# A distance table made on VectorE instead of by GpSimd's iota, constant warm-up operands, diagonals shared with ScalarE, and a new order

## The chip, the cores and the metric

The kernel runs on one core of one Trainium2 chip. The time is the device time of one launch in microseconds (us), given as the median of the runs. Engines are named as in the profile: PE (TensorE matmul), PEld (its weight load), DVE (VectorE), ACT (ScalarE), POOL (GpSimd), SP (SyncE).

## The reference

Local attention with a few global keys and a distance bias, over q, k, v of shape (4, 8, 768, 64), and then a token-mixing layer over its output, of shape (4, 768, 512):

```python
scores = scale * np.matmul(q, k.transpose(0, 1, 3, 2))
rel = pos[:, None] - pos[None, :]
is_global = pos[None, :] < 8
is_local = (rel >= 0) & (rel < 96)
keep = is_global | is_local
dist = np.where(is_global & ~is_local, 96.0, np.abs(rel))
slopes = 2.0 ** (-8.0 * (np.arange(H) + 1) / H)
scores = np.where(keep, scores - slopes * dist, -1e9)
x = softmax(scores) @ v                      # heads side by side: (4, 768, 512)

theta = x @ w_theta
y = w_tok_r @ (x * cos(theta)) + w_tok_i @ (x * sin(theta))    # over tokens
u = x + y
out = u + np.maximum(u @ w_ch, 0)
```

## The kernel before

Tokens are cut into six tiles of 128, heads into four pairs. A query tile meets only its own key tile and the one before, in which the eight global keys replace the first eight columns (`kG` for K, `vG` for V). For each batch and pair the steps are: `q`/`qq` transposes of Q and K on PE and `qe` copies out of PSUM (on ACT or DVE, as the order says), `kg` (L360, L361), `s` scores on PE (L409), `e` the exponential on ACT (L421), `v` the product with V on PE (L468), whose 65th column is a column of ones and so gives the row sum, and `n`, reciprocal and multiplication on DVE (L479, L481). `xt` or a DMA transposes the result. The second half follows per batch: `th` (theta, L534), `sn` (cosine and sine on ACT, L544 and L546), `z` (products on DVE, L555), `m` (token mixing on PE, L568), `u`, its transpose, `c` (L617), `r` (L627) and the stores.

The bias enters in two ways. In batch 0 it is added by PE before the scores: `sb` (L382, L389) multiplies `diag`, the identity times a head's slope (L148), by `dist`, a table of 128 by 6 by 128 distances. In the later batches the exponential is multiplied on DVE by `etab`, a table of exp(-slope * distance) that ACT makes per head (`bt`, L153); so all eight tables are needed only from batch 1 on.

`dist` and `ident` come from `near`, whose element (p, j) is j - p. In the kernel before, GpSimd writes `near` with an iota (L106). VectorE makes `ident` (L120) and, in `distances` (L127 to L135), `far`, then `near` with the masked places put far away, their maximum as `dist`, two copies of it and the places of the global keys. `swap` (L141, L142) makes `distS`, `dist` with its halves swapped.

Batch 0 is loaded at the start. The first pair of heads comes in f32 over SP's and ACT's queues (L103, into `qk32`) and is cast by ACT and DVE (`cast`, L288). The rest comes over GpSimd's queue, which casts on the way: q and k of heads 2 and 3, then of 4 and 5, then V of heads 0 to 3 (`vn`, L92), q and k of 6 and 7, then V of heads 4 to 7. `vn` has 65 columns per head and tile: the loads write 64, and a memset on DVE writes the column of ones (L112). Before the loads of later batches the same memset stands as `mv` (L212).

PE also runs warm-ups (`warm`, L237): matmuls of a tile of zeros, written by DVE (L109), whose results nothing reads.

Nothing is scheduled by a program when the kernel is built. A text, `order`, names every step after the start in one sequence (L641 to L706), and each engine runs its own steps in that sequence; `banks` gives the PSUM bank of each. The start of the kernel (L101 to L157) stands in the order of the source. A build then adds the waits that the reads and writes of each tile ask for. An engine's instructions start in their order, so one that waits holds all behind it on its engine.

Of the kernel before, what the change touches and what calls it, by code (L numbers as in the profile page):

```python
# [16 lines left out]
def kernel(  # L17
# [47 lines left out]
    loads = {}  # L65
# [40 lines left out]
    nc.gpsimd.iota(near, pattern=[[1, 2 * T]], base=0, channel_multiplier=-1,  # L106
                   allow_small_or_imprecise_dtypes=True)
    zero = const.tile([T, 512], BF)
    nc.vector.memset(zero, 0.0)  # L109
    alloc_qk(0)  # L110
    alloc_v(0)
    nc.vector.memset(loads[0][1][:, :, :, D:D + 1], 1.0)  # L112
# [11 lines left out]
    far = const.tile([T, 2 * T], FP)  # L124
# [122 lines left out]
    @op  # L247
    def diag_(p):
        diagonals(p)
# [386 lines left out]
    def do(op, *a):  # L636
# [10 lines left out]
        s.0.1.2 sb.1.1 e.0.1.0 kg.0.2.0.4.v s.0.1.1 lw.2 vg.0.0.4 sb.2.0 e.0.1.2 sb.2.1 s.0.2.1
        e.0.1.1 v.0.0.0.0.6 s.0.2.0 n.0.0.0.0.6 lq.1.0.8 q.0.3.1 e.0.2.0 q.0.3.0 qe.0.3.1.v.2
        v.0.0.1.0.6 qe.0.3.0.a.2 sb.2.2 n.0.0.1.0.6 sb.3.0 e.0.2.1 v.0.1.0.0.6 kg.0.3.0.4.v
        v.0.1.1.0.6 n.0.1.0.0.6 s.0.2.2 sb.3.1 e.0.2.2 vg.0.4.4 s.0.3.0 s.0.3.1 e.0.3.0 n.0.1.1.0.6  # L650
        v.0.2.1.0.6 v.0.2.0.0.6 e.0.3.1 lw.4 n.0.2.1.0.6 v.0.3.2.0.2 xt.0.1.0.6 xt.0.0.0.6
        n.0.3.2.0.2 v.0.3.2.2.4 xe.0.0.0.6.a n.0.2.0.0.6 sb.3.2 s.0.3.2 xe.0.1.0.6.v e.0.3.2
        xt.0.2.0.6 xt.0.3.0.2 th.0.0.4 xe.0.2.0.6.v xe.0.3.0.2.a n.0.3.2.2.4 lc th.0.0.5 mv.1
        xt.0.3.2.4 v.0.3.2.4.6 xe.0.3.2.4.v th.0.0.3 n.0.3.2.4.6 th.0.1.2 sn.0.0.0 lv.1.4.4 sn.0.0.1
        xt.0.3.4.6 th.0.1.3 xe.0.3.4.6.v ww.0 sn.0.1.0 lv.1.0.4 ww.1 we.0.0.v th.0.2.2 we.1.0.v
        sn.0.1.1 z.0.0.1 lq.2.0.8 we.1.1.a th.0.2.3 z.0.0.0 ww.2 we.0.1.v ww.3 we.2.0.a z.0.1.1
        m.0.1.0 we.2.1.a z.0.1.0 m.0.0.0 sn.0.2.0 we.3.1.v m.0.2.0 sn.0.2.1 z.0.2.0 m.0.0.1 sin.0
        z.0.2.1 m.0.1.1 pc.1.0.0 m.0.0.2 pc.1.1.0 we.3.0.v bt.7 m.0.1.2 bt.2 pc.1.0.1 pc.1.1.1
        qq.1.0 u.0.0 qq.1.1 qe.1.0.1.a.2 u.0.1 m.0.3.0 qe.1.1.1.a.2 kg.1.0.0.4.v ud.0.1 ut.0.0
        qe.1.0.0.v.2 m.0.3.1 qe.1.1.0.a.2 ue.0.0.a kg.1.1.0.4.v s.1.0.0 pc.1.2.0 s.1.0.1 e.1.0.0  # L660
        pc.1.2.1 ww.4 pc.1.3.0 m.0.2.2 we.4.0.v e.1.0.1 we.4.1.v s.1.1.0 x.1.0.0 qq.1.2 e.1.1.0
        s.1.0.2 x.1.0.1 m.0.3.2 e.1.0.2 x.1.1.0 m.0.2.1 qe.1.2.1.a.2 u.0.3 s.1.1.1 mv.2 qe.1.2.0.a.2
        s.1.1.2 pc.1.3.1 m.0.4.0 kg.1.2.0.4.v lv.2.0.8 e.1.1.2 x.1.0.2 u.0.2 e.1.1.1 s.1.2.0 s.1.2.2
        m.0.4.2 x.1.1.2 e.1.2.0 x.1.1.1 lq.3.0.4 m.0.4.1 e.1.2.2 x.1.2.0 ut.0.2 ww.5 u.0.4 ue.0.2.a
        qq.1.3 we.5.1.a x.1.2.2 s.1.2.1 c.0.2.2 vg.1.0.8 we.5.0.a c.0.1.2 e.1.2.1 r.0.2.2
        v.1.0.2.0.6 qe.1.3.0.a.2 x.1.2.1 ut.0.3 qe.1.3.1.a.2 n.1.0.2.0.6 m.0.5.0 kg.1.3.0.4.a ut.0.4
        v.1.2.2.0.6 r.0.1.2 xd.1.0 ue.0.3.a v.1.1.2.0.6 n.1.2.2.0.6 ue.0.4.a s.1.3.0 c.0.3.2 e.1.3.0
        pc.2.1.0 pc.2.0.0 n.1.1.2.0.6 m.0.5.2 bt.6 s.1.3.1 r.0.3.2 s.1.3.2 e.1.3.1 xt.1.2.0.6
        x.1.3.0 xt.1.1.0.6 m.0.5.1 e.1.3.2 x.1.3.1 c.0.0.2 xe.1.2.0.6.a x.1.3.2 pc.2.1.1
        xe.1.1.0.6.a v.1.3.2.0.6 pc.2.0.1 u.0.5 qq.2.0 n.1.3.2.0.6 qq.2.1 qe.2.0.0.a.2 c.0.4.2  # L670
# [6 lines left out]
        ud.1.1 qe.2.2.0.a.2 u.1.0 s.2.1.1 vg.2.0.8 s.2.0.1 s.2.0.2 m.1.2.2 e.2.0.2 kg.2.2.0.4.v
        e.2.1.1 m.1.2.1 x.2.1.0 e.2.0.1 s.2.2.0 u.1.2 s.2.1.2 c.0.5.2 x.2.0.2 e.2.1.2 ud.1.2 x.2.1.1
        m.1.3.0 e.2.2.0 r.0.5.2 pd.3.2.1 s.2.2.2 x.2.0.1 qq.2.3 e.2.2.2 s.2.2.1 x.2.1.2 m.1.3.2
        e.2.2.1 st.0.2.2 x.2.2.2 pd.3.1.0 v.2.1.2.0.6 qe.2.3.0.a.2 m.1.5.0 n.2.1.2.0.6 qe.2.3.1.a.2  # L680
        v.2.0.2.0.6 kg.2.3.0.4.a x.2.2.0 xd.2.1 m.1.5.1 n.2.0.2.0.6 s.2.3.1 s.2.3.0 m.1.5.2 x.2.2.1
        e.2.3.0 xd.2.0 m.1.3.1 e.2.3.1 u.1.5 v.2.2.2.0.6 u.1.3 c.1.1.2 kg.3.0.0.4.v n.2.2.2.0.6
        m.1.4.0 x.2.3.0 s.3.0.0 s.2.3.2 ud.1.3 r.1.1.2 m.1.4.2 e.2.3.2 x.2.3.1 e.3.0.0 c.1.2.2
        xd.2.2 x.2.3.2 kg.3.1.0.4.a v.2.3.2.0.6 m.1.4.1 pd.3.2.0 n.2.3.2.0.6 c.1.3.2 u.1.4 xd.2.3
        th.2.0.0 vg.3.0.4 th.2.1.0 r.1.3.2 st.0.3.2 th.2.0.6 ud.1.0 th.2.2.0 th.2.0.3 st.1.3.2
        th.2.1.6 sn.2.0.0 pd.3.3.1 th.2.2.6 sn.2.0.1 th.2.1.3 z.2.0.0 c.1.0.2 st.0.1.2 sn.2.1.0
        z.2.0.1 pd.3.3.0 th.2.2.3 m.2.1.0 sin.3 sn.2.1.1 z.2.1.0 ud.1.4 m.2.0.0 sn.2.2.0 z.2.1.1
        m.2.2.0 r.1.2.2 st.1.1.2 sn.2.2.1 z.2.2.0 m.2.1.1 st.0.4.2 r.1.0.2 m.2.2.1 z.2.2.1
# [61 lines left out]
```

## Time and profile before

| what | value |
|---|---|
| median of 3 runs | 162.62 us (161.27 to 163.02) |
| the profiled execution: its time | 162.9 us |
| its span, first to last instruction | 160.7 us |
| mean granted TensorE clock | 0.999 |
| bytes moved by DMA | 25.49 MB, mean 159 GB/s |

Busy time by stage, in us of the engine's own time:

| stage (us) | PE | DVE | ACT | POOL |
|---|---|---|---|---|
| 0 to 10 | 7.82 | 6.30 | 6.25 | 9.19 |
| 10 to 20 | 9.37 | 8.78 | 8.90 | 5.38 |
| 20 to 30 | 9.38 | 7.51 | 9.22 | 5.20 |
| 30 to 40 | 9.79 | 8.79 | 9.11 | 0.88 |
| 60 to 70 | 9.95 | 9.67 | 9.04 | 5.90 |
| 70 to 80 | 8.92 | 9.90 | 8.06 | 3.68 |
| 140 to 150 | 9.95 | 4.04 | 0.00 | 0.00 |
| 150 to 161 | 7.30 | 5.69 | 0.59 | 0.00 |

A row of the timeline gives the start and the length in us, the engine, the line of the kernel, the operation with the tile that it writes and the tiles that it reads, their shape, and how many instructions are merged in it. Brackets give the idle time of the engine before it and what ended that time. In the list of waits a row names who waited for whom: us in total, times, and the longest. [...]

### The profile page before, as it was taken

What the parts mean: (1) busy time and instruction counts of PE and PEld (TensorE: products, weight loads), DVE (VectorE), ACT (ScalarE), POOL (GpSimd) and SP (SyncE); (2) the same over time, 40 slices, a digit from 0 to 9 for tenths busy, and PEclk for the clock granted to TensorE, in tenths of its full rate; (3) what the DMA queues carried; (4) which work ended last, traced back from release to release, by engine and by line L of the source; (5) the groups of instructions that cost most, each with busy time, mean ns of one, the idle gap of its engine ahead of it and who ended that gap; (6) DMA issues with size and microseconds to landing.
All of it is one profiled execution on the core that took longest, in us unless ns stands there. A gap on an engine that the chain in (4) does not pass through costs nothing.

```text
span 160.7 us, 4144 instructions
## 1 busy us (share of the span) xinstructions
PE 151.4 (94%) x1717; PEld 82.5 (51%) x1741; DVE 124.8 (78%) x263; ACT 107.4 (67%) x141; POOL 38.4 (24%) x46
## 2 busy tenths in 40 slices
PE   5989989999999999997999999999999999999991
PEld 1355774645546757444456554445465544444470
DVE  7578895897999999999998874697799715733492
ACT  3879898998999887998697391988963057200010
POOL 7985435400049320993000000000000000000000
PEclk9999999999999999999999999999999999999999
DMA  4999999999999999999998456953263470098376
GB/s 140 208 171 176 206 209 205 204 208 205 156 165 203 184 143 147 134 129 154 157 128 206 93 98 147 229 167 63 57 191 64 85 197 4 0 364 193 65 263 227
DMA packets 73553, 25.49 MB, mean 159 GB/s; under 512 B 61376, under 2 KB 70848, under 8 KB 73536
## 3 DMA queue, kind: packets, MB, share of 16 engines
q0 software_dynamic: 45712, 12.45, 84.5%
q1 hardware_dynamic: 27120, 12.00, 33.5%
q10 hardware_dynamic: 704, 0.79, 1.4%
q8 instruction: 13, 0.21, 0.5%
q14 instruction: 4, 0.03, 0.1%
HBM read 25.69 MB, written 6.29 MB: 199 GB/s over the span
## 4 chain that ended last, share of the span: by engine, by line
PE 80%; DVE 13%; issue 2%; ACT 2%; POOL 0%; DVEq 0%; POOLq 0%
PE bank L568 37%; PE bank L617 12%; PE bank L534 10%; PE bank L468 6%; PE bank L409 6%; PE bank L312 3%; PE bank L382 2%; DVE kT L337 2%; DVE x_sb L481 2%; DVE zri L555 2%; DVE qkn L344 1%; PE bank L498 1%; DVE o L627 1%; PE bank L237 1%; PE bank L303 1%
## 5 line engine op out<-in xcount | busy, mean ns | idle before, releaser
L568 PE MATMUL bank<-zri,w_tokT 128*128 128x512 bf16 x273 | 66.6, 379 | 2.1 <-DVE zri L555 1.0
L421 ACT ACTIVATE e<-bank 128x1024 bf16<-128x1024 f32 (+1 forms) x48 | 42.9, 959 | 8.9 <-PE bank L409 7.6
L568 PEld LDWEIGHTS <-w_tokT 128*128 128x128 bf16 x288 | 26.5, 98 | 30.9 <-issue 1.4
L555 DVE TENSOR_TENSOR zri<-x_sb,cs 128x1024 bf16<-128x1024 bf16 (+1 forms) x30 | 16.5, 579 | 9.6 <-ACT cs L546 7.2
L617 PE MATMUL bank<-w_ch_bf,uT 128*128 128x512 bf16 (+1 forms) x103 | 23.6, 355 | 0.3
L534 PE MATMUL bank<-w_theta_bf,xT 128*128 128x512 bf16 x93 | 22.5, 379 | 0.2
L627 DVE SCALAR_TENSOR_TENSOR o<-bank,u 128x512 f32<-128x512 f32 (+1 forms) x27 | 16.7, 625 | 6.0 <-PE bank L617 5.8
L576 DVE TENSOR_TENSOR u<-x_sb,bank 128x512 bf16<-128x512 bf16 x24 | 16.4, 682 | 4.1 <-PE bank L568 4.1
L546 ACT ACTIVATE cs<-bank,halfpi 128x1024 bf16<-128x1024 f32 x8 | 8.9, 1112 | 12.3 <-PE bank L534 12.1
L481 DVE TENSOR_TENSOR x_sb<-bank,rec 128x768 bf16<-128x768 f32 (+2 forms) x21 | 16.1, 767 | 0.7
L430 DVE TENSOR_TENSOR e<-e,etab 128x1024 bf16<-128x1024 bf16 (+1 forms) x24 | 14.6, 619 | 1.5 <-ACT e L421 1.2
L617 PEld LDWEIGHTS <-uT 128*128 128x128 bf16 x108 | 10.1, 98 | 9.3
L409 PE MATMUL bank<-qT,kT 64*128 64x128 bf16 x224 | 14.0, 218 | 0.5 <-DVE kT L337 0.3
L534 PEld LDWEIGHTS <-xT 128*128 128x128 bf16 x96 | 9.1, 98 | 10.2 <-DMA xT<-x_sb 0.3
L92 POOL DMA_DIRECT2D vn<-in_v_dram x6 | 10.2, 1708 | 16.9 <-DVE kG L361 13.7
L468 PEld LDWEIGHTS <-e 128*128 128x128 bf16 x352 | 12.6, 97 | 3.3 <-issue 0.8
L606 ACT COPY uT<-bank 128x512 bf16<-128x512 bf16 x5 | 2.9, 592 | 17.1 <-PE bank L592 17.0
L468 PE MATMUL bank<-vn,e 128*128 128x65 bf16 x224 | 13.3, 193 | 0.0
L409 PEld LDWEIGHTS <-kT 64*128 64x128 bf16 x224 | 8.8, 94 | 8.5 <-issue 6.9
L409 PE MATMUL bank<-qT,kG 64*128 64x128 bf16 x128 | 10.8, 216 | 0.4 <-DVE kG L361 0.4
L468 PE MATMUL bank<-vG,e 128*128 128x65 bf16 x128 | 10.3, 193 | 0.4 <-DVE vG L445 0.4
L433 DVE TENSOR_TENSOR e<-e,etab 128x1024 bf16<-128x1024 bf16 x12 | 8.2, 684 | 0.5 <-ACT e L421 0.3
(79 smaller groups left out, 185.2 us busy)
## 6 DMA issues: line engine op xcount, KB each, us to landing
out_dram<-o SPq DMA_DIRECT2D x21, 256.0 KB, 2.4
vn<-in_v_dram POOLq DMA_DIRECT2D x4, 384.0 KB, 16.0
qk<-in_q_dram POOLq DMA_DIRECT2D x2, 768.0 KB, 20.4
qk<-in_k_dram POOLq DMA_DIRECT2D x2, 768.0 KB, 21.1
vn<-in_v_dram POOLq DMA_DIRECT2D x2, 768.0 KB, 15.9
w_nat<-in_moe_w_tok_r_dram POOLq DMA_DIRECT2D x3, 384.0 KB, 12.1
w_nat<-in_moe_w_tok_i_dram POOLq DMA_DIRECT2D x3, 384.0 KB, 13.3
qk<-in_q_dram POOLq DMA_DIRECT2D x8, 96.0 KB, 8.5
```

Source lines behind the costliest of these rows:

```text
L92: nc.gpsimd.dma_start(out=vn[:, h0:h0 + n, :, 0:D].rearrange("p h t d -> p (h t) d"), in_=v[b, h0:h0 + n].rearrange("h (t p) d -> p (h t) ...
L409: nc.tensor.matmul(pb[:, hh, o:o + T], lhsT=lhsT, rhs=qT[R, (own, nxt)[part]], start=fresh, stop=fresh or (jt == NT - 1 or (j == 1 and par ...
L421: nc.scalar.activation(e_c, ps_of["s", b, p, c][:, :, 0:blocks(c) * T], AF.Exp, scale=scale)
L430: nc.vector.tensor_mul(e_c, e_c, tab[:, :, s0:s0 + n].rearrange("p a s n -> p a (s n)"))
L468: nc.tensor.matmul(po4[:, head - h0, it - i0], lhsT=l_, rhs=r_, start=(i_ == 0), stop=(i_ == len(mms) - 1))
L481: nc.vector.tensor_mul(xv, po4[:, :, :, 0:D], rec.to_broadcast([T, m_, nt, D]))
L534: nc.tensor.matmul(ps_of["th", b, c][j_], lhsT=xT_sb[b][:, dc, (2 * c + j_) * T:(2 * c + j_ + 1) * T], rhs=w_theta_bf[:, dc, :], start=(dc ...
L555: nc.vector.tensor_mul(zri[b][:, i_, tt, :].rearrange("p j (g d) -> p j g d", g=NP), x_sb[b][:, :, tt, :].rearrange("p g j d -> p j g d"), ...
L568: nc.tensor.matmul(ps_of["m", b, tt], lhsT=w_tokT[wi][:, st, tt * T:(tt + 1) * T], rhs=zri[b][:, wi, st, :], start=(mixed[b, tt] == 0), st ...
L576: nc.vector.tensor_add(u_sb[b, tt].rearrange("p (g d) -> p g d", g=NP), x_sb[b][:, :, tt, :], ps_of["m", b, tt].rearrange("p (g d) -> p g ...
L617: nc.tensor.matmul(ps, lhsT=uTs[b, tt][:, dc, :], rhs=w_ch_bf[:, dc, own], start=(dc == 0), stop=(dc == NC - 1))
L627: nc.vector.scalar_tensor_tensor(o_sbs[b, tt][:, own], in0=ps_of["c", b, tt, part], scalar=0.0, in1=u_sb[b, tt][:, own], op0=ALU.max, op1= ...
```

## The change

- The iota and the memset of `zero` go. DVE makes the same table: a running sum over constant ones starts at -1 and gives the ramp 0, 1, 2, ... along the free axis in every partition (`ramp`, in the buffer of `far`); a transpose of the first 32 columns (in blocks of 32 by 32) gives each partition its number within its block (`lane`); three additions of 32, 64 and 96 make it the partition's number; `ident` is `ramp` equal to `lane`, and `near` is `ramp` minus `lane`.
- The memset of `vn`'s column of ones moves from ahead of batch 0's loads to behind them and behind these steps.
- The warm-ups multiply constant ones, which the program's preamble holds, with a stride of 0. There are ten of them, not eleven, and all stand ahead of the first `sb`.
- `diag` gets an engine: pairs 1 and 2 are made on ACT, pairs 0 and 3 on DVE.
- The order is written anew, with new banks. The steps are the same but for the warm-ups, and some change their engine: batch 0's first K copies and the first Q copies change places between DVE and ACT, some `xe`, `kg`, `qe`, `we` and `ue` steps change sides. Three more bias tables (`bt`) stand behind the last sines of batch 0 instead of in the first 10 us.

In the compiled program the moved memset is DVE's eighth instruction, behind the running sum, the transpose, the three additions, `ident` and `near`. It waits for the completion of both loads of `vn`. In the program before it was DVE's second instruction and waited for nothing; the first `vn` load waited for it.

The code, without the long order:

```diff
-    near = const.tile([T, 2 * T], FP)
-    nc.gpsimd.iota(near, pattern=[[1, 2 * T]], base=0, channel_multiplier=-1,
-                   allow_small_or_imprecise_dtypes=True)
-    zero = const.tile([T, 512], BF)
-    nc.vector.memset(zero, 0.0)
+    ones = nc.const_aps.tensor(1.0, [T, 512], BF)
+    ones32 = nc.const_aps.tensor(1.0, [T, 2 * T], FP)
     alloc_qk(0)
     alloc_v(0)
-    nc.vector.memset(loads[0][1][:, :, :, D:D + 1], 1.0)
     load_qk(0, 2, 2)
     load_qk(0, 4, 2)
     load_v(0, 0, 4)
     load_qk(0, 6, 2)
     load_v(0, 4, 4)
 
+    ramp = far = const.tile([T, 2 * T], FP, name="far")
+    lane = const.tile([T, GS], FP)
+    near = const.tile([T, 2 * T], FP)
+    nc.vector.tensor_tensor_scan(ramp, ones32, ones32, -1.0, op0=ALU.mult, op1=ALU.add)
+    nc.vector.transpose(lane, ramp[:, 0:GS])
+    for r in range(GS, T, GS):
+        nc.vector.tensor_scalar(lane[r:r + GS, 0:1], lane[r:r + GS, 0:1], float(r), None, op0=ALU.add)
     ident = const.tile([T, T], BF)
-    nc.vector.tensor_scalar(ident, near[:, 0:T], 0.0, None, op0=ALU.is_equal)
+    nc.vector.tensor_scalar(ident, ramp[:, 0:T], lane[:, 0:1], None, op0=ALU.is_equal)
+    nc.vector.tensor_scalar(near, ramp, lane[:, 0:1], None, op0=ALU.subtract)
+    nc.vector.memset(loads[0][1][:, :, :, D:D + 1], 1.0)
...
-    def diagonals(p):
+    def diagonals(p, eng):
         for h in (2 * p, 2 * p + 1):
-            nc.vector.tensor_scalar(diag[:, h], ident, -slopes[h] / scale, None, op0=ALU.mult)
+            if eng == "a":
+                nc.scalar.mul(diag[:, h], ident, -slopes[h] / scale)
+            else:
+                nc.vector.tensor_scalar(diag[:, h], ident, -slopes[h] / scale, None, op0=ALU.mult)
...
-            nc.tensor.matmul(ps, lhsT=zero[:, 0:T], rhs=zero, start=True, stop=True)
+            nc.tensor.matmul(ps, lhsT=ones[:, 0:T], rhs=ones, start=True, stop=True)
...
-        warm.1.3 diag.3 warm.3.1 dist warm.1.2 diag.0 bt.0 sb.0.0 sb.0.1 cast.0.1.a cast.0.0.v
-        warm.6.0 cast.1.1.a bt.4 cast.1.0.v bt.1 q.0.1.0 swap q.0.0.0 bt.3 q.0.0.1 diag.1
+        warm.3.1 warm.6.0 diag.0.v dist bt.5 warm.1.2 cast.1.0.v sb.0.1 cast.1.1.a cast.0.1.a
+        diag.3.v diag.1.a q.0.0.1 cast.0.0.v qe.0.0.1.a.0 swap q.0.0.0 qe.0.0.1.a.1 q.0.1.0
...
-        m.0.1.0 we.2.1.a z.0.1.0 m.0.0.0 sn.0.2.0 we.3.1.v m.0.2.0 sn.0.2.1 z.0.2.0 m.0.0.1 sin.0
-        z.0.2.1 m.0.1.1 pc.1.0.0 m.0.0.2 pc.1.1.0 we.3.0.v bt.7 m.0.1.2 bt.2 pc.1.0.1 pc.1.1.1
+        m.0.1.0 sn.0.2.1 we.2.0.v z.0.2.0 m.0.0.1 sin.0 z.0.2.1 m.0.1.1 we.3.1.v we.2.1.v bt.2
+        m.0.0.2 we.3.0.v bt.6 pc.1.1.0 m.0.1.2 u.0.0 bt.0 pc.1.0.0 m.0.2.0 bt.1 bt.3 pc.1.0.1
...
-        sn.1.1.0 r.0.4.2 m.1.1.0 sn.1.1.1 z.1.1.0 th.1.2.3 m.1.0.0 sn.1.2.0 z.1.1.1 m.1.1.1 ue.0.5.v
-        kg.2.0.1.4.v sn.1.2.1 pd.3.1.1 pc.2.3.1 m.1.0.1 z.1.2.0 z.1.2.1 qq.2.2 pd.3.0.1 s.2.1.0
+        pc.2.2.0 pc.2.2.1 sn.1.1.1 z.1.1.0 th.1.2.3 m.1.0.0 sn.1.2.0 z.1.1.1 m.1.1.1 r.0.3.2
+        sn.1.2.1 pd.3.1.1 z.1.2.0 m.1.0.1 sin.1 ue.0.5.a z.1.2.1 qq.2.2 st.0.3.2 s.2.1.0
```

More of the change, by code (lines that the diff above doesn't have):

```diff
@@ L247, in diag_ @@
     @op
-    def diag_(p):
-        diagonals(p)
+    def diag_(p, eng="v"):
+        diagonals(p, eng)
     @op
@@ L647 @@
[L647 to L652, printed above, removed]
@@ L659 @@
[L659 to L664, printed above, removed]
@@ L665 @@
[L665 to L670, printed above, removed]
@@ L677 @@
[L677 to L682, printed above, removed]
@@ L683 @@
[L683 to L688, printed above, removed]
@@ new lines @@
+        diag.3.v diag.1.a q.0.0.1 cast.0.0.v qe.0.0.1.a.0 swap q.0.0.0 qe.0.0.1.a.1 q.0.1.0
+        qe.0.0.0.v.0 sb.0.2 qe.0.1.0.a.2 qe.0.0.0.v.1 q.0.1.1 kg.0.0.0.1.v lt.0.2 kg.0.0.1.4.v
+        sb.0.0 qe.0.1.1.v.2 s.0.0.0 lt.2.4 s.0.0.2 e.0.0.0 q.0.2.0 lw.0 kg.0.1.0.4.v q.0.2.1
+        qe.0.2.0.v.2 s.0.0.1 e.0.0.2 sb.1.0 qe.0.2.1.v.2 diag.2.a s.0.1.0 sb.1.1 e.0.0.1
+        kg.0.2.0.4.v s.0.1.1 sb.2.0 e.0.1.0 vg.0.0.4 sb.1.2 lw.2 s.0.2.0 e.0.1.1 s.0.1.2 v.0.0.0.0.6
+        q.0.3.0 n.0.0.0.0.6 e.0.1.2 v.0.0.1.0.6 lq.1.0.8 v.0.1.0.0.6 qe.0.3.0.v.2 e.0.2.0 q.0.3.1
@@ new lines @@
+        e.3.1.1 m.2.0.2 n.3.0.2.0.6 e.3.2.0 m.2.4.0 u.2.0 s.3.3.2 vg.3.4.4 s.3.2.2 ud.2.0 s.3.3.0
+        e.3.2.2 m.2.4.1 x.3.1.1 e.3.3.0 x.3.1.0 ud.2.1 m.2.4.2 x.3.2.0 e.3.3.2 c.1.4.2 x.3.2.2
+        xd.3.0 u.2.4 s.3.1.2 s.3.2.1 e.3.1.2 s.3.3.1 r.1.4.2 m.2.5.0 ud.2.4 e.3.3.1 x.3.1.2
+        v.3.1.2.0.6 x.3.3.2 e.3.2.1 m.2.5.1 n.3.1.2.0.6 m.2.5.2 x.3.3.0 xd.3.1 m.2.3.0 x.3.3.1
+        x.3.2.1 v.3.3.2.0.6 st.1.4.2 v.3.2.2.0.6 c.2.1.2 n.3.2.2.0.6 c.2.0.2 r.2.1.2 xd.3.2 c.1.5.2
+        n.3.3.2.0.6 m.2.3.1 r.1.5.2 xd.3.3 m.2.3.2 r.2.0.2 th.3.0.0 st.1.5.2 u.2.3 th.3.2.0 ud.2.2
@@ new lines @@
+        th.3.0.6 th.3.1.0 st.1.3.2 th.3.0.3 st.2.0.2 th.3.1.6 ud.2.3 sn.3.0.0 c.2.2.2 sn.3.0.1
+        z.3.0.0 th.3.1.3 th.3.2.6 sn.3.1.0 z.3.0.1 c.2.4.2 r.2.2.2 sn.3.1.1 th.3.2.3 r.2.4.2 m.3.2.0
+        sn.3.2.0 z.3.1.0 m.3.0.0 sn.3.2.1 z.3.2.0 m.3.1.0 u.2.5 c.2.3.2 z.3.1.1 ud.2.5 z.3.2.1
+        m.3.1.1 r.2.3.2 m.3.0.2 m.3.2.2 m.3.0.1 m.3.4.0 u.3.0 m.3.3.0 ud.3.0 m.3.1.2 st.2.2.2
+        c.2.5.2 u.3.1 st.2.3.2 st.2.4.2 m.3.2.1 ud.3.1 m.3.4.2 u.3.2 r.2.5.2 m.3.3.1 ud.3.2 m.3.4.1
+        c.3.0.2 u.3.4 m.3.5.0 ud.3.4 r.3.0.2 m.3.3.2 st.2.1.2 m.3.5.1 u.3.3 st.2.5.2 m.3.5.2 ud.3.3
@@ L710 @@
+        21654206306420463064034064263564062351056226420426126402146327467215415302313276540132
     """.split())]
```

73 lines of the change are left out of this document (42 added, 31 removed).

## The prediction

> **What bounds the kernel now.** I read four views in this order: the page's busy shares, the waits of all engines, the timeline of the first 20 us by engine, and busy time by stage. The page says that TensorE carries the kernel:
>
> ```profile
> PE 151.4 (94%) x1717; PEld 82.5 (51%) x1741; DVE 124.8 (78%) x263; ACT 107.4 (67%) x141; POOL 38.4 (24%) x46
> ```
>
> 151.4 of 160.7 us. Nearly all of PE's idle time lies before 25 us and behind the last matmul at 156. Between them the table by stage has PE at 8.9 to 9.95 of every 10 us, so nothing there can take in a late start. The waits name one gap in the middle, on VectorE's `zri` (next fence). Of the start the reader needs four things from the timeline.
>
> ```profile
> POOL qk L77 <- DMA vn<-in_v_dram: 2.5, 1, 2.5
> ...
> POOL w_nat L168 <- DMA vn<-in_v_dram: 1.9, 1, 1.9
> ...
> PE bank L568 <- DVE zri L555: 1.0, 1, 1.0
> ```
>
> First, GpSimd's queue. It holds the iota, then eight loads of batch 0; the two `vn` loads are the fifth and the eighth. Their landing is seen where later loads wait for them:
>
> ```profile
> 0.84 0.33 POOL L106 IOTA near<- 128x256 f32 x1 [0.39 <-POOLq L731]
> 1.35 0.84 POOL L77 DMA_DIRECT2D qk<-in_q_dram  x1 [0.18 <-issue]
> ...
> 4.32 1.45 POOL L92 DMA_DIRECT2D vn<-in_v_dram  x1
> ...
> 7.16 1.45 POOL L92 DMA_DIRECT2D vn<-in_v_dram  x1
> ...
> 13.34 0.72 POOL L168 DMA_DIRECT2D w_nat<-in_moe_w_tok_r_dram  x1 [1.88 <-DMA vn<-in_v_dram]
> ...
> 18.18 0.88 POOL L77 DMA_DIRECT2D qk<-in_k_dram  x1 [2.50 <-DMA vn<-in_v_dram]
> ```
>
> The view of DMA issues gives 8.7 us from issue to landing for the first `vn` load and 10.7 for the second: the second lands at 7.16 + 10.7 = 17.9 us, and what waits for it goes on at 18.18. Second, VectorE, which today sets `vn`'s column of ones (L112) before those loads are issued and waits for nothing there:
>
> ```profile
> 1.26 0.10 DVE L112 MEMSET vn<- 128x48 bf16 x1
> ...
> 1.68 0.29 DVE L127 TENSOR_SCALAR far<-near 128x256 f32<-128x256 f32 x1
> ...
> 3.71 0.18 DVE L135 TENSOR_SCALAR dist<-dist 8x128 bf16<-8x128 bf16 x1
> ...
> 5.26 0.96 DVE L288 CAST qkn<-qk 128x384 bf16<-128x384 f32 x2 [0.91 <-DMA qk<-in_q_dram]
> 6.25 0.40 DVE L141 COPY distS<-dist 64x768 bf16<-64x768 bf16 x1
> ```
>
> Third, this engine does not pass a waiting instruction: L141 needs only `dist`, complete at 3.89, yet ran at 6.25, behind the casts that waited 0.91 us for their data. Fourth, all early work hangs on this stretch: ScalarE's first bias table (L153) waits 1.4 us for `dist`, and PE's first useful matmul (L382, 4.05) for `diag`.
>
> **The change, part by part.** *The memset of `vn`* decides. In the new text it stands behind the two `vn` loads, and in the compiled order of the changed kernel VectorE's eighth instruction, this memset, carries two waits that it did not have: for the completion of both loads. The loads write columns 0 to 63 of `vn` and the memset column 64, but they share a tile. Queued behind it on VectorE are `halfpi`, two diagonals, the whole distance chain (L127 to L135), two casts and the swap. ScalarE's first instruction behind its table load is a bias table, which needs `dist`; PE has only ten warm-ups before its first bias product. Everything waits for the second `vn` load.
>
> When that lands: with the iota gone GpSimd starts its loads at 0.84, not 1.35, and none of the eight waits, so the second `vn` load is issued 0.51 earlier, at 6.65; with the same 10.7 it lands at 17.35. If the DMA engines, at 9 tenths from 3 us on, pass on none of the 0.51, it is 17.9, and with the lag of today's waiter 18.2. I take 17.5, near the row's own latency. From the memset's start to `dist`'s end the rows give 3.89 - 1.26 = 2.63, so `dist` is complete at 20.1 in place of 3.89: **+16.2 us** (16.1 to 16.9).
>
> *Running sum, transpose, three additions, subtraction* on VectorE replace iota (0.33, POOL) and the memset of `zero` (0.27). The trace has no scan and no transpose on VectorE. Nearest rows: 128x256 f32 with two inputs 0.42 (L128), the bound from above twice that; transpose and each addition between 0.06 (memset 128x1) and 0.23 (L120). Scan 0.42 to 0.85, the other four 0.24 to 0.92, `ident` 0.23, `near` 0.29 (L127): they end between 2.0 and 3.2 us, far under 17.5. Cost nothing; cover the wait itself, and without it about 1.4 us, since `dist` would end at some 5.3.
>
> *Warm-ups on constant ones*: PE need not wait for `zero` (1.2 us in the waits) and starts about 0.3 us earlier; ten matmuls, 0.43 apart as the five of the first L237 row are (2.32), end near 5.2. They lie beside the wait and gain nothing.
>
> *`dist` to the first exponential* (first e row at 10.58, 6.7 us behind `dist`). After the wait the inputs have landed, so the 0.91 of the cast and the six warm-ups between the bias products and the transposes (2.02) are gone. Chain by rows: bias table 0.74, two casts on ScalarE 0.92, two diagonals there some 0.5 (estimate from the 0.37 of a 128x256 copy), PE's K and Q transposes, Q's two halves on VectorE 1.02, `kG` 0.36, five further PE steps. With PE at full speed 4.9 us. Later matmuls start 0.216 apart (L568, four in 0.86), though the granted clock stands at 1.00 in the first stages too; after an idle stretch from 5.2 to 20 I take the slow spacing again, for 0.8 more: 5.7. That is **-1.0** (-1.8 to -0.4). [...]
>
> *First exponential to first sine* (26.39, 15.8 later). Summing rows over both order lists, ScalarE gains 1.0 of work there (one xT copy and two diagonals come, three bias tables go), VectorE loses 1.2. Both were about nine tenths busy: **0** (-1 to +1).
>
> *Bias tables moved* behind the last sines: five in a row in place of two, 3 x 0.68 = 2.04 more on ScalarE before batch 1's K is copied out. Of it 0.56 falls into today's idle time, and 0.76 is repaid because two `w_tokT` copies (1.50) leave ScalarE ahead of it and two short xT copies (0.74) come. PE, in order, then waits before batch 1's scores: **+0.7** (0 to 2.0).
>
> *The gap at 74.5*: VectorE ran `uT` (0.42), `kG` (0.64) and a 2.19 `qkn` copy, which lay beside GpSimd's `vn` issue (71.39, 2.29; the same copy's median is 0.35), in front of the last two `zri` products. The new order has the first two on ScalarE and the copy earlier: **-1.0** (-1.0 to 0).
>
> *All other moves of the order* keep the same matmuls, transposes and stores. PE has 9.8 or more in nearly every 10 us from 80 to 150, with some 4 us of slack by matmul counts; the tail keeps its six half-width products and stores: **0** (-0.5 to +1.5).
>
> Sum: 16.2 - 1.0 + 0 + 0.7 - 1.0 + 0 = +14.9. The profiled execution took 162.9 (span 160.7 and 2.2 around it), 0.3 over the median of 162.62; it would come to 177.8, and the median to **177.5**.
>
> **Rivals.** *The wait costs nothing.* It decides at a point: if the memset ran by about 3.7 us, the rest would be no slower than before. Then the first e would start near 9.4 (1.2 earlier), and -1.2 + 0.7 - 1.0 gives 161.1. For it: the bytes do not overlap. [...] It would need the build's waits not to hold. [...]
>
> *Lost time is won back behind the wait.* PE's useful matmuls before 31.6 us come to about 21 us (counts by spacing), so a third of today's head is waiting; if the landed loads and idle GpSimd sped VectorE's copies (`kG` rows 0.28 alone, 0.40 to 0.64 beside GpSimd), at most 2 to 3 us return: 175. Against: after 10 us no wait of ScalarE or VectorE in the list is for a load.
>
> *PE stays slow longer.* Today the slow spacing lasts from 1.19 to about 6.7. If as much lasts from 20.1, with PE feeding two full engines, another 2.5 us: 180. Against: PE has slack beside them there.
>
> **How the numbers follow.** Forecast (176 to 179) 0.68; won back 0.14; slow longer 0.14; wait free 0.02; the order's remainder worse than its bounds 0.02. The range takes in the forecast and both neighbours: 174 to 181. Within 1% means within 1.6 us, about what runs from 161.27 to 163.02 can tell apart. Only the free wait is faster or the same: faster 0.01, same 0.02, slower 0.97.
>
> **What would show it.** VectorE idle before the `vn` memset for some 15 us, released by the `vn` load, near 17.5; `dist`'s end near 20; PE idle from about 5 to 20; matmuls 0.43 apart behind it; no gap on `zri` near 89; the same 2.2 us around the span. I am wrong if the memset runs before 4 us, or if the span grows by much less than the memset's delay: then the head had slack that I did not see.

## The result and the profile after

The changed kernel took 175.31 us (median of 4 runs, 175.11 to 175.72), the kernel before 161.94 us beside it (4 runs, 160.9 to 163.02). The ratio is 1.0814, with a 95% interval from 1.0751 to 1.0878. The profiled execution took 175.39 us, of which 173.3 are its span.

The page of the profile shows where the time did not go. Its first part (busy time, share of the span, instructions) and its clock row (40 slices, tenths of full speed):

```profile
PE 154.6 (89%) x1740; PEld 83.3 (48%) x1740; DVE 122.5 (71%) x263; ACT 106.6 (61%) x146; POOL 38.4 (22%) x45
...
PEclk9955559999999999999999999999999999999999
```

TensorE was busy 3.2 us longer than before (a rough figure: the trace of before has 1717 of its matmuls, this one 1740, though the change has one fewer), VectorE 2.3 less, ScalarE 0.8 less; TensorE's share fell from 94% to 89%. The span is 12.6 us longer, and idle time grew by 9.4 us on TensorE, 14.9 on VectorE and 13.4 on ScalarE. The list of waits shows where, in one stretch:

```profile
ACT etab L161 <- DVE dist L140: 17.3, 1, 17.3
DVE diag L156 <- DMA vn<-in_v_dram: 14.7, 1, 14.7
...
PE bank L390 <- DVE dist L139: 14.5, 1, 14.5
```

VectorE waits 14.7 us for a `vn` load, and TensorE and ScalarE wait for `dist`. The timeline of VectorE from the start (start, length, engine, line, operation, shapes, idle time before it and its releaser):

```profile
0.78 0.69 DVE L119 TENSOR_TENSOR_SCAN far<-const-float32-1.0 128x256 f32<-128x256 f32 x1 [0.78 <-PEq L739]
1.50 0.21 DVE L120 STREAM_TRANSPOSE lane<-far 128x32 f32<-128x32 f32 x1
1.75 0.46 DVE L122 TENSOR_SCALAR lane<-lane 32x1 f32<-32x1 f32 x3
2.25 0.28 DVE L124 TENSOR_SCALAR ident<-far,lane 128x128 bf16<-128x128 f32 x1
2.45 0.43 DVE L125 TENSOR_SCALAR near<-far,lane 128x256 f32<-128x256 f32 x1
17.62 0.29 DVE L156 TENSOR_SCALAR diag<-ident 128x128 bf16<-128x128 bf16 x2 [14.73 <-DMA vn<-in_v_dram]
17.76 0.10 DVE L126 MEMSET vn<- 128x48 bf16 x1
...
19.31 0.23 DVE L138 COPY dist<-dist 128x256 bf16<-128x256 bf16 x1
19.46 0.22 DVE L139 COPY dist<-dist 128x256 bf16<-128x256 bf16 x1
19.59 0.18 DVE L140 TENSOR_SCALAR dist<-dist 8x128 bf16<-8x128 bf16 x1
```

The new table is ready at 2.88 us and then lies there until 17.62. The bracket stands on a diagonal, which needs no `vn`; in the program the memset (L126) is ahead of it, though its record begins at 17.76. The instruction that waited is the memset: the chain that ended last (second fence below: start, length, what; DVEq is VectorE's own queue) has L126 between the load's landing and the diagonal. GpSimd's timeline and this chain show how long the load took:

```profile
1.24 0.81 POOL L77 DMA_DIRECT2D qk<-in_q_dram  x1 [0.80 <-POOLq L739]
...
7.00 1.49 POOL L92 DMA_DIRECT2D vn<-in_v_dram  x1
...
17.74 0.88 POOL L77 DMA_DIRECT2D qk<-in_k_dram  x1 [2.22 <-DMA vn<-in_v_dram]
```

```profile
7.00 10.46 DMA vn<-in_v_dram
...
17.48 0.02 DVEq L126
...
17.62 0.24 DVE diag L156
```

The second `vn` load is issued at 7.00 and lands at 17.46. Now the transfer is itself on the chain that ended last; before the change it was hidden.

The landmarks below are starts or ends of rows in the four timelines (us). "Memset first" and "iota back" are experiments told further on; the last column is that of the fastest kernel. The profile of "memset first" is of the slowest of its twelve runs (161.35 us); a second reading of the same kernel, profiled in a run of 159.77 us, has `dist` complete at 5.90 and a span of 157.9.

| landmark | before | after | memset first | iota back, second reading |
|---|---|---|---|---|
| `dist` complete | 3.89 | 19.77 | 5.91 | 3.89 |
| first exponential | 10.58 | 26.09 | 11.66 | 9.45 |
| first sine, batch 0 | 26.39 | 40.84 | 27.03 | 24.71 |
| batch 1's first scores | 40.62 | 55.27 | 41.46 | 39.15 |
| first sine, batch 1 | 65.97 | 80.49 | 66.67 | 64.52 |
| first sine, batch 2 | 99.76 | 112.75 | 98.93 | 96.78 |
| first sine, batch 3 | 130.10 | 143.54 | 129.72 | 127.57 |
| span | 160.7 | 173.3 | 159.5 | 157.3 |

### The profile page after: what moved, and what is told of

Its sections match the earlier page's. It is cut to its first block, busy times and chain, and to the rows that moved or that the text cites. A ratio compares the mean times of both kernels' runs of the same rounds, so it can differ in the third digit from the quotient of the medians.

```text
span 173.3 us, 4174 instructions
## 1 busy us (share of the span) xinstructions
PE 154.6 (89%) x1740; PEld 83.3 (48%) x1740; DVE 122.5 (71%) x263; ACT 106.6 (61%) x146; POOL 38.4 (22%) x45
## 4 chain that ended last, share of the span: by engine, by line
PE 84%; DMA 6%; POOL 3%; DVE 3%; issue 1%; ACT 0%; DVEq 0%; POOLq 0%
PE bank L576 37%; PE bank L542 12%; PE bank L625 11%; PE bank L417 7%; PE bank L476 6%; DMA vn<-in_v_dram 6%; PE bank L320 3%; PE bank L311 3%; POOL qk L77 2%; PE bank L390 2%; DVE o L635 1%; PE bank L506 1%; PE bank L397 1%; PE bank L600 1%; POOL vn L92 1%
## 5 line engine op out<-in xcount | busy, mean ns | idle before, releaser
L576 PE MATMUL bank<-zri,w_tokT 128*128 128x512 bf16 x288 | 67.7, 379 | 0.0
L584 DVE TENSOR_TENSOR u<-x_sb,bank 128x512 bf16<-128x512 bf16 x24 | 16.2, 683 | 11.1 <-PE bank L576 11.1
L92 POOL DMA_DIRECT2D vn<-in_v_dram x6 | 10.2, 1702 | 33.2 <-DVE rec L487 18.0
L390 PE MATMUL bank<-dist,diag 128*128 128x512 bf16 (+1 forms) x12 | 4.6, 474 | 14.5 <-DVE dist L139 14.5
L161 ACT ACTIVATE etab<-dist 128x640 bf16<-128x640 bf16 x8 | 5.4, 727 | 17.3 <-DVE dist L140 17.3
L417 PE MATMUL bank<-qT,kT 64*128 64x128 bf16 x224 | 13.4, 219 | 0.1
L156 DVE TENSOR_SCALAR diag<-ident 128x128 bf16<-128x128 bf16 x4 | 0.6, 201 | 14.7 <-DMA vn<-in_v_dram 14.7
```

The costliest lines, as they stand in the source:

```text
L92: nc.gpsimd.dma_start(out=vn[:, h0:h0 + n, :, 0:D].rearrange("p h t d -> p (h t) d"), in_=v[b, h0:h0 + n].rearrange("h (t p) d -> p (h t) ...
L417: nc.tensor.matmul(pb[:, hh, o:o + T], lhsT=lhsT, rhs=qT[R, (own, nxt)[part]], start=fresh, stop=fresh or (jt == NT - 1 or (j == 1 and par ...
L576: nc.tensor.matmul(ps_of["m", b, tt], lhsT=w_tokT[wi][:, st, tt * T:(tt + 1) * T], rhs=zri[b][:, wi, st, :], start=(mixed[b, tt] == 0), st ...
L584: nc.vector.tensor_add(u_sb[b, tt].rearrange("p (g d) -> p g d", g=NP), x_sb[b][:, :, tt, :], ps_of["m", b, tt].rearrange("p (g d) -> p g ...
```

## The experiments

Each ratio is to the kernel before, run beside it on the same chip, with its 95% interval. The theory: all of the loss is the memset's place; `dist` waits for the second `vn` load, and the span grows by as much as `dist` is late. The rivals: the running sum or the new order cost time; TensorE's clock after the idle stretch does.

**Undo one line.** The changed kernel, with the memset where it was:

```diff
     alloc_v(0)
+    nc.vector.memset(loads[0][1][:, :, :, D:D + 1], 1.0)
     load_qk(0, 2, 2)
...
-    nc.vector.memset(loads[0][1][:, :, :, D:D + 1], 1.0)
```

> The changed kernel with the vn memset ahead of batch 0's loads again; nothing else. Theory A (the wait of VectorE for the second vn load is the whole loss): the 14.7 us of idle time before VectorE's first diagonal go, dist is complete near 5.3 us, the time comes to 160 to 162 us, ratio to the kernel before 0.985 to 1.005. Rival B (the new start or the new order costs by itself, and the wait only hides it): the time stays above 163 us.

Measured: 160.67 us (159.81 to 161.35), ratio 0.9933 [0.9902, 0.9965]. The whole loss goes with this line, and what remains of the change is a little faster than the kernel before. From this kernel to the changed one `dist` moves by 13.86 us (5.91 to 19.77), the profiled span by 13.8 (159.5 to 173.3) and the median by 14.6.

**Do one line alone.** The kernel before, with nothing but that memset moved behind the loads:

```diff
-    nc.vector.memset(loads[0][1][:, :, :, D:D + 1], 1.0)
     load_qk(0, 2, 2)
...
     load_v(0, 4, 4)
+    nc.vector.memset(loads[0][1][:, :, :, D:D + 1], 1.0)
```

> The kernel before with only the vn memset moved behind batch 0's loads (iota, old order and all else kept). Theory A: VectorE waits until the second vn load lands, some 17.9 us, dist is complete near 20.5 in place of 3.89, and the time comes to 175 to 179 us. Rival B: a good part of the loss belongs to the rest of the change, and this one takes under 172 us.

Measured: 180.05 us (179.19 to 180.33), ratio 1.114 [1.1083, 1.1198]. The line alone costs more than the whole change, and one microsecond more than the upper end that was expected. Its list of waits shows the same picture:

```profile
PE bank L382 <- DVE diag L148: 17.6, 1, 17.6
...
DVE ident L120 <- DMA vn<-in_v_dram: 17.0, 1, 17.0
```

Here `ident` stands behind the memset too, and `dist` is complete at 20.95. It moves by 17.06 us against the kernel before, the span by 17.4. In the changed kernel the running sum, `ident` and `near` are done while VectorE would otherwise wait. That and a later landing make 1.2 us of the 4.8 between the two spans (178.1 and 173.3); the other 3.6 lie behind `dist`, 2.1 of them between the first sines of batches 1 and 2 (34.37 here, 32.26 in the changed kernel), where the two kernels differ by their order.

**Wait for half.** The changed kernel, with the memset cut in two by heads. Heads 4 to 7, which the second load fills, get their ones ahead of the loads; heads 0 to 3 get theirs late, so that only the first `vn` load is waited for:

```diff
     alloc_v(0)
+    nc.vector.memset(loads[0][1][:, 4:8, :, D:D + 1], 1.0)
...
-    nc.vector.memset(loads[0][1][:, :, :, D:D + 1], 1.0)
+    nc.vector.memset(loads[0][1][:, 0:4, :, D:D + 1], 1.0)
```

> The changed kernel with the memset split by heads: heads 4 to 7 (the second vn load) ahead of the loads, heads 0 to 3 at the late place, so that VectorE waits for the first vn load alone. Theory A: the load lands 4.6 us earlier (its waiter goes on at 13.18 against 17.74), so the time falls by 4 to 5 us to about 170.5. Rival C (what costs is not the length of the wait but something that follows any such stall, such as the slow clock or cold queues): falls by less than 2 us.

Measured: 170.82 us (170.04 to 171.77), ratio 1.058 [1.0518, 1.0642], as expected. `dist` is complete at 14.99 and the span is 167.9. So the loss follows the load that is waited for. With the two kernels around it, `dist` at 5.91, 14.99 and 19.77 gives spans of 159.5, 167.9 and 173.3, and medians of 160.67, 170.82 and 175.31. So the first 9.08 us of delay cost 8.4 us by the profiles and 10.2 by the medians, the next 4.78 cost 5.4 and 4.5: one for one to within about 1 us.

**Keep TensorE warm through the wait.** Sixty warm-ups where one stood, so 69 in all:

```diff
-        warm.3.1 warm.6.0 diag.0.v dist bt.5 warm.1.2 cast.1.0.v sb.0.1 cast.1.1.a cast.0.1.a
+        warm.3.1 warm.6.0 diag.0.v dist bt.5 warm.60.2 cast.1.0.v sb.0.1 cast.1.1.a cast.0.1.a
```

> The changed kernel with 69 warm-ups in place of 10, so that PE runs matmuls until about 19 us while VectorE waits. Theory A with PE's slow start on the path behind the wait: transposes and bias products start at full speed, the first exponential comes 0.7 to 1.2 us earlier than 26.1, and the time falls by 0.5 to 1.2 us to about 174.4. Rival D (ScalarE and VectorE set the pace behind the wait, PE has slack): within 0.3 us of the changed kernel.

Measured: 175.32 us (174.64 to 176.53, 4 runs), ratio 1.0864 [1.0802, 1.0927]. In the profile, of a run of 174.64 us whose mean granted clock is 1.00, the first exponential came 4.28 us behind `dist` instead of 6.32, but the median did not follow. The changed kernel had not run on that chip, so both were run together:

> The changed kernel once more, unchanged, beside the next one on the same chip: 174.5 to 176 us.

> The kernel with 69 warm-ups once more, beside the changed kernel on the same chip, because its first look was split: the first exponential came 1.7 us earlier, the span was 0.8 us shorter, the median the same. Theory A (the slow clock behind the wait costs most of a microsecond at the end): 0.5 to 1 us under the changed kernel. Rival D (won in the head, given back by the middle): within 0.3 us.

Measured: the changed kernel 175.29 us (174.59 to 176.01, 6 runs), ratio 1.082 [1.0765, 1.0875]; with the warm-ups 176.03 us (175.69 to 176.34, 6 runs), ratio 1.0859 [1.0808, 1.0911]. The warm-ups gain nothing. TensorE's timeline of this second reading names two places (the row at 108.83 stands ahead of the wait):

```profile
19.77 0.59 PE L390 MATMUL bank<-dist,diag 128*128 128x512 bf16 x2 [2.37 <-DVE dist L139]
...
108.83 2.75 PE L542 MATMUL bank<-w_theta_bf,xT 128*128 128x512 bf16 x11
112.42 2.33 PE L542 MATMUL bank<-w_theta_bf,xT 128*128 128x512 bf16 x10 [0.84 <-DMA xT<-x_sb]
```

First, the warm-ups ended 2.37 us too early, and the granted clock still fell to 0.63 between 20 and 22.5 us; all six runs have a mean clock of 0.99. (In the profile of the first reading, which kept its clock, they ended 1.56 us too early.) Second, the 0.8 us by which batch 1's scores came earlier (54.56 against 55.35), half of which is an earlier `dist` (19.81 against 20.21), were used up at 112, where batch 2's theta waits for a transpose by DMA. That wait is in both profiles with the warm-ups and in neither profile of the changed kernel. What a kernel would gain whose clock never falls is not settled by these runs.

**The iota back.** With the memset first, the table from GpSimd's iota again, and the new order, the constant warm-ups and the diagonals on ScalarE kept:

```diff
+    near = const.tile([T, 2 * T], FP)
+    nc.gpsimd.iota(near, pattern=[[1, 2 * T]], base=0, channel_multiplier=-1,
+                   allow_small_or_imprecise_dtypes=True)
...
-    nc.vector.tensor_tensor_scan(ramp, ones32, ones32, -1.0, op0=ALU.mult, op1=ALU.add)
-    nc.vector.transpose(lane, ramp[:, 0:GS])
...
-    nc.vector.tensor_scalar(ident, ramp[:, 0:T], lane[:, 0:1], None, op0=ALU.is_equal)
-    nc.vector.tensor_scalar(near, ramp, lane[:, 0:1], None, op0=ALU.subtract)
+    nc.vector.tensor_scalar(ident, near[:, 0:T], 0.0, None, op0=ALU.is_equal)
```

> The kernel with the memset first (160.67 us), with GpSimd's iota in place of the running sum, transpose, additions and subtraction; new order kept. Theory (the running sum delays the distance table, the iota costs GpSimd's queue only 0.1 us, as the first loads start at 1.24 without it and 1.35 with it): dist complete near 3.9 in place of 5.9 us, first exponential 1 to 2 us earlier than 11.66, time 159.3 to 160.2 us. Rival (ScalarE and VectorE behind it set the pace, the head takes the 2 us back): within 0.3 us of 160.67.

Measured: 159.73 us (159.6 to 160.75), ratio 0.9867 [0.9817, 0.9917]. This is faster than the kernel before and the changed kernel, and within what was expected.

**The old order.** With the memset first and the running sum kept, the `order` and `banks` of the kernel before, with all diagonals on VectorE:

```diff
-        warm.3.1 warm.6.0 diag.0.v dist bt.5 warm.1.2 cast.1.0.v sb.0.1 cast.1.1.a cast.0.1.a
+        warm.1.3 diag.3.v warm.3.1 dist warm.1.2 diag.0.v bt.0 sb.0.0 sb.0.1 cast.0.1.a cast.0.0.v
...
```

> The kernel with the memset first, running sum and constant warm-ups, but the order, banks and diagonals on VectorE of the kernel before. Theory (the new order is what gains, by the gap on zri at 74.5 us above all, and the running sum costs): 162 to 163.5 us, the gap of about 1 us on zri is there. Rival (the gain of the memset-first kernel is the running sum's or the warm-ups'): 160 to 161 us.

Measured: 165.01 us (163.89 to 165.54), ratio 1.0171 [1.0113, 1.023], above what was expected. TensorE's timeline shows why the old order takes the later table worse:

```profile
6.07 1.89 PE L390 MATMUL bank<-dist,diag 128*128 128x512 bf16 x4 [3.00 <-DVE diag L156]
7.75 2.61 PE L245 MATMUL bank<-const-bfloat16-1.0 128*128 128x512 bf16 x6
```

TensorE waits 3.00 us for a diagonal that VectorE makes behind the table (0.54 in the kernel before), and six warm-ups stand behind the bias products in front of the first transposes. With five warm-ups ahead and six behind, a late table costs the idle time and 2.61 us of useless work after it (2.02 in the kernel before); the new order has all ten ahead. The gap on `zri` is there, but less than half as long as expected, the kernel before first:

```profile
74.52 2.92 PE L568 MATMUL bank<-zri,w_tokT 128*128 128x512 bf16 x11 [0.97 <-DVE zri L555]
```

```profile
76.27 2.92 PE L576 MATMUL bank<-zri,w_tokT 128*128 128x512 bf16 x11 [0.43 <-DVE zri L563]
```

"The one line alone", which has the old order too, waits 0.71 us there; no profile with the new order has the wait in its list.

**The running sum on one chip.** The earlier readings with and without the iota came from different chips, so the two kernels ran together:

> The changed kernel with the memset of `vn` ahead of the loads, once more, beside the same with the iota back. What is told apart: whether the running sum itself costs time once nothing hides it. Theory: it does; its table was complete at 5.91 us against 3.89 with the iota, and the two earlier readings came from different chips (0.9933 and 0.9867 of the kernel before), so on one chip the running sum's version should stand 1.0 to 1.5 us above the iota's. Rival: the difference was the chips', and the two stand within 0.3 us.

> The new order with the iota and with the memset ahead of the loads, on the same chip as the run before it. Theory: 1.0 to 1.5 us under that run, near 159.7. Rival: within 0.3 us of it.

Measured: with the running sum 160.31 us (159.76 to 161.14, 12 runs), ratio 0.9931 [0.9892, 0.9971]; with the iota 159.60 us (159.25 to 160.11, 6 runs), ratio 0.9887 [0.9837, 0.9938]. The means differ by 0.70 us, with a 95% interval of 0.45 either way from the spread of the runs. The running sum does cost time when nothing hides it, less than the 1.0 to 1.5 expected. Three of its twelve runs have a mean clock of 0.989 and took 160.96 to 161.14 us, which none of the six with the iota does; without them the difference is 0.48 us (0.4 either way). TensorE's first bias products in the two profiles, the running sum's first:

```profile
5.81 0.59 PE L390 MATMUL bank<-dist,diag 128*128 128x512 bf16 x2 [0.60 <-DVE dist L139]
```

```profile
5.00 1.06 PE L385 MATMUL bank<-dist,diag 128*128 128x512 bf16 x2
```

With the running sum `dist` is complete at 5.90 and TensorE waits for it; with the iota it is complete at 3.89 and TensorE does not. The first exponential comes 0.74 us later (10.19 against 9.45).

**The gap at 74.5.** The fastest kernel with one place of the old order back: VectorE does three steps ahead of the last `zri` products again, two of which the new order had given to ScalarE:

```diff
-        qe.2.1.1.a.2 mv.3 ut.0.5 kg.2.0.1.4.a pc.2.3.0 xt.1.3.0.6 kg.2.0.0.1.v th.1.0.0 r.0.4.2
-        xe.1.3.0.6.a qe.2.1.0.v.2 th.1.0.6 th.1.0.3 kg.2.1.0.4.v th.1.1.0 pc.2.3.1 sn.1.0.0 th.1.2.0
+        qe.2.1.1.a.2 mv.3 ut.0.5 pc.2.3.0 xt.1.3.0.6 kg.2.0.0.1.v th.1.0.0 r.0.4.2
+        xe.1.3.0.6.a qe.2.1.0.v.2 th.1.0.6 th.1.0.3 kg.2.1.0.4.v th.1.1.0 sn.1.0.0 th.1.2.0
...
-        sn.1.2.1 pd.3.1.1 z.1.2.0 m.1.0.1 sin.1 ue.0.5.a z.1.2.1 qq.2.2 st.0.3.2 s.2.1.0
+        sn.1.2.1 pd.3.1.1 ue.0.5.v kg.2.0.1.4.v pc.2.3.1 z.1.2.0 m.1.0.1 sin.1 z.1.2.1 qq.2.2 st.0.3.2 s.2.1.0
```

> The kernel of the run before with one edit of the order taken back: VectorE does batch 0's last `ue` update, `kg.2` and the first output accumulation ahead of `z.1.2.0` again, as in the kernel before. Theory: this is where the gap of 0.97 us on `zri` at 74.52 came from; TensorE waits on `zri` again for about 1 us near 72 to 73 us, and the time is 0.8 to 1.5 us above the run before it. Rival: the wait comes back and is taken up later by slack ahead of batch 2; time within 0.3 us.

Measured: 160.48 us (159.91 to 161.26, 12 runs), ratio 0.9927 [0.9891, 0.9964]. The mean is 0.85 us above that of the kernel without the edit (95%: 0.45 either way), within what was expected; the wait that was to show it did not come. TensorE's timeline has another in its place:

```profile
72.77 2.06 PE L571 MATMUL bank<-zri,w_tokT 128*128 128x512 bf16 x8
75.10 1.02 PE L571 MATMUL bank<-zri,w_tokT 128*128 128x512 bf16 x4 [0.28 <-DVE qT L335]
```

The eight matmuls start 0.216 us apart, so the ninth could start at 74.50; it starts at 75.10, when VectorE's copy of `qT` ends and frees a PSUM bank. Here VectorE's delay arrives at TensorE through the next thing that it owes, not through `zri`. This profile shows 0.62 us between the first sines of batches 1 and 2 (32.88 against 32.26); another 0.92 of its longer span lies ahead of batch 1's sine, and ahead of the edit, where the first reading of the kernel without the edit was 0.64 later as well (65.16). So some 0.6 us of the price are read from the profile and 0.85 are measured for the edit as a whole, and the wait of 0.97 us on `zri` was not made again by it alone: the `qkn` copy that took 2.19 us in the kernel before, ahead of the last `zri` products, took 0.65 here.

## Why the prediction was right, and where its sizes were off

The direction, the mechanism and its place were right; the time of 177.5 us was 2.2 too high. The measured 175.31 lies inside the range of 174 to 181, but below the forecast's own 176 to 179 (chance 0.68), beside the 175 of a rival (0.14); that the number was caught is owed to a range that took the neighbours in. The terms, as profiled execution against profiled execution:

| step of the prediction | predicted | measured | from |
|---|---|---|---|
| memset wait, to `dist` complete | +16.2 | +15.88 | 3.89 to 19.77 |
| `dist` to first exponential | -1.0 | -0.37 | 6.69 to 6.32 |
| first exponential to first sine | 0 | -1.06 | 15.81 to 14.75 |
| bias tables, to batch 1's scores | +0.7 | +0.20 | 14.23 to 14.43 |
| gap on `zri`, batch 1's sine to batch 2's | -1.0 | -1.53 | 33.79 to 32.26 |
| all other moves | 0 | -0.52 | 86.29 to 85.77 |
| sum, span | +14.9 | +12.6 | 160.7 to 173.3 |

Only the bias tables' term lies inside its own bounds; the other five lie outside theirs by 0.02 to 0.53 us, four of them on the low side. So the bounds of the single terms were too narrow, and the deviations added up to 2.3 us.

The time around the span stayed, at 2.1 us for 2.2. The profiled execution of before, at 162.9, lies in the upper part of its runs, so medians differ a little more than profiles: 13.4 us.

*The memset wait* came as told: idle 14.73 us, released by the `vn` load, `dist` at 19.77 for 20.1. Taking the iota away let GpSimd start its loads 0.11 us earlier (1.24 for 1.35), not 0.51: the wait of 0.80 us at its start is there without the iota too. The load was issued at 7.00 instead of 6.65, but took 10.46 us for 10.7, and landed at 17.46 for 17.35. From the memset to `dist` the chain took 2.15 us for 2.63 (17.62 to 19.77), for two reasons. From the start of the first copy of `dist` to the table's end it took 0.46 for 0.73, as the two copies, which overlap, took 0.23 and 0.22 with no load being issued on GpSimd (none between 19.32 and 19.70), against 0.51 and 0.43 beside its issues before; and `far` began 0.21 behind the first row instead of 0.42.

*The running sum* was free behind the wait, as predicted. Without it `dist` is complete at 5.9, not at the 5.3 given, and the price is 0.70 us, not 1.4. Of the 0.6 us between 5.9 and 5.3 the copies, at 0.89 and 0.81 (last section), make 0.37, and `far`, at 0.51 for 0.29, makes the rest. The scan took 0.69 us, between the two bounds of 0.42 and 0.85, and 1.6 times the 0.42 of the two-input row of the same shape; the upper bound, twice that row, was an estimate that no row of before supports.

*`dist` to the first exponential* was mis-sized twice, and the errors partly cancel. The first reading with 69 warm-ups shows the stretch at a granted clock of 1.00: 4.28 us for the 4.9 given. No run shows the 0.8 us that was added for the slow spacing behind an idle stretch: it was an estimate, and in its place the changed kernel's 6.32 is 2.04 longer than that 4.28, as TensorE stayed slow longer than was allowed. Its timeline, 24 transposes of the same shape twice:

```profile
20.67 1.81 PE L311 MATMUL bank<-ident,qkn 128*64 128x128 bf16 x24
...
26.15 0.86 PE L311 MATMUL bank<-ident,qk 128*64 128x128 bf16 x24
```

The granted clock is 0.50 from 10 us to 25 and 0.84 from 25 to 27.5, so that it rose near 25.8 if it rose in one step, and nearly the whole chain to the first exponential, at 26.09, runs under 0.50. The rise came some 6 us after work began at 19.73. The fall was earlier: the warm-ups end at 5.20, and the mean clock of 0.87 from 5 to 10 us puts it near 8.7, some 3.5 us behind their end, again if it was one step. What sets either time is not shown by these runs; in the trace of before a mean clock of 0.999 leaves no room for such a stretch. In the kernel that waits for half, whose `dist` is 4.78 us earlier, the mean clock of the profiled run is 0.970, against 0.949.

*First exponential to first sine* was put at 0 and was -1.06. With the memset first and the iota back, so with the new order and no wait, it is -0.55 (15.81 to 15.26); with the one line alone, so with the wait and the old order, it is -0.57 (15.81 to 15.24). So half is the order and half the wait. That the half of the wait comes from batch 0's inputs having landed is likely, but not shown.

*The bias tables* cost 0.20 of the 0.7, near the lower end given; which work of TensorE covers the five tables was not tested. *The gap* is gone, and the stretch gained 1.53, half a microsecond more than the gap itself. *All other moves* gained 0.52 where nothing was given: sine to sine of batches 2 and 3 lost 0.45 (30.34 to 30.79), the stretch behind that gained 0.84 (30.6 to 29.76). The kernel with the iota back has both (30.79 and 29.73), the one with the old order neither (30.35 and 30.53), so they are the order's.

The rivals. *The wait costs nothing* fell: the memset waited. *Lost time is won back behind the wait* gave 175, closest to the time, but for 2 to 3 us where the runs show about 0.8: 0.27 us in the copies of `dist` and 0.57 before the first sine. The rest of what was missing came mostly from the order, so the nearness of its number is in part luck. *TensorE stays slow longer* was right about the clock and too high in its price. At the first exponential the slow clock costs 2.04 us, 1.2 more than the forecast had, where the rival had 2.5 more. What is left of it at the end of the kernel stays open. One run of the changed kernel in its second reading has a mean clock of 1.00 and took 174.59 us, the other five, at 0.947 to 0.951, 175.17 to 176.01; the two runs with 69 warm-ups at 1.00 in the first reading took 174.64 and 175.03, the two at 0.99 took 175.61 and 176.53. But of the four runs that wait for half, the one at 1.00 took 171.40, longer than two at 0.97 (170.04 and 170.24). And a recorded clock of 1.00 did not go with full speed everywhere here. With the one line alone it is 1.00 in all runs, yet the first four bias products behind the wait take as long as the slow ones of the kernel before (1.89 us at 4.05; two of them take 0.60 at 27.27 in the changed kernel):

```profile
21.10 1.89 PE L382 MATMUL bank<-dist,diag 128*128 128x512 bf16 x4 [17.59 <-DVE diag L148]
```

What the change is worth without its misplaced line, by the four kernels that set the ones first: against the old order with the iota, which is the kernel before, the old order with the running sum has a ratio of 1.0171 [1.0113, 1.023], the new order with the running sum 0.9931 [0.9892, 0.9971] and the new order with the iota 0.9887 [0.9837, 0.9938]. The new order gains, the running sum loses, and the version to keep is the new order with the iota and the ones set ahead of the loads, at 159.60 us.

## What to carry to other kernels

Before moving a step, list every tile that it writes, and who else is writing that tile at its new place: here ones in a column that no load touches still waited 14.7 us for the loads of the others, and with the ones of heads 0 to 3 alone the memset ran at 12.92 in place of 17.76. A waiting instruction costs what is queued behind it on its engine, here the table that three engines needed, and the price can be read beforehand: issue time plus latency of the transfer that it would wait for, less the time at which it ran (here 16.2 us by the prediction; undoing the line gave back 14.6, and the line alone cost 18.7). When a delay or a gain is predicted on an engine, look for it at the next thing that this engine owes to the bottleneck, which may be a bank and not the tile that one had in mind. When several small terms are added, keep the range of the sum wider than their bounds suggest: here five of six left theirs, if by little.

## What the runs showed of the hardware that was not expected

Some of VectorE's copies within SBUF took longer beside an issue of a load on GpSimd (0.89 us for 0.23), and at one place the issue took longer too (1.21 for 0.74). The kernel with the memset first shows both in its timeline:

```profile
4.81 0.89 DVE L138 COPY dist<-dist 128x256 bf16<-128x256 bf16 x1
...
5.60 1.21 POOL L77 DMA_DIRECT2D qk<-in_q_dram  x1
```

The copy took 0.23 us with GpSimd idle, 0.51 beside GpSimd's issues in the kernel before, and 0.89 here (0.88 in the second reading). Not every issue lengthened it: with the one line alone the same copy took 0.23 inside an issue (20.43, the issue from 20.18 to 20.90). The load's issue took 1.21 us here, 1.20 in the second reading, and 0.74 at the same place of the changed kernel, where VectorE stood still. So a step that was moved by 1.65 us went from 0.51 to 0.89. The longest case is the `qkn` copy of the kernel before:

```profile
71.68 2.19 DVE L344 COPY qkn<-qk 128x768 bf16<-128x768 bf16 x1
```

It began inside a load's issue (71.39 to 73.68) and ended 0.19 us behind the issue's end. In the changed kernel a `kG` copy (L368, 128x512) began inside a `vn` load's issue too (79.59, the issue from 78.26 to 80.48) and ended 0.09 behind its end, after 0.98 us; the same copy at 28.64, with no load being issued, took 0.29. The 0.89 of the first row also ends 0.05 behind the end of an issue (4.19 to 5.65). This is read from their lying side by side; no run took the issues away alone.

A short idle stretch in the first 10 us goes with a lower clock in some runs and not in others of the same kernel. TensorE's timeline in the first reading with the memset first:

```profile
0.78 3.78 PE L245 MATMUL bank<-const-bfloat16-1.0 128*128 128x512 bf16 x10 [0.78 <-PEq L739]
5.82 0.59 PE L390 MATMUL bank<-dist,diag 128*128 128x512 bf16 x2 [1.26 <-DVE dist L139]
```

Here the warm-ups ended early, TensorE waits 1.26 us and, near 7 us, another 0.56, and the granted clock is 0.90 from 4 to 8 us and 0.68 from 8 to 12. In the second reading's profile the warm-ups took 4.43 us, the waits are 0.60 and 0.56, and the mean clock of the run is 1.00. The two profiles with 69 warm-ups differ the same way: 1.56 us of idle time at a mean clock of 1.00, 2.37 with the dip to 0.63. That the longer idle time makes the dip is read from these two pairs, not shown by a run of its own. In the first reading six of twelve runs had a mean clock of 0.989 and took 160.75 to 161.35 us (mean 161.00); the other six, at 0.996 or more, took 159.81 to 160.58 (mean 160.18). In the second, three of twelve had 0.989 (mean 161.02, the other nine 160.15). So the runs at 0.989 took 0.8 to 0.9 us longer, more than the running sum costs in the others (0.48).
